# A TensorE loop whose leftover pairs become a short last round, ended by a branch

## The chip, the cores and the metric

One core of one Trainium2 chip. The metric is the device time of one execution in microseconds (us). "Before" and "after" are the kernel without and with the change. Times quoted for a kernel are medians of its fast runs. A ratio is the mean time of one kernel's fast runs over that of the other's of the same rounds, so it is not quite the ratio of the medians; each comes with a 95% interval.

## The reference, cut to what matters

```python
# x: (1, 512, 512, 192) bf16;  w: (1, 1, 4, 48, 48) bf16
xg = x.reshape(1, 512, 512, 4, 48)
out = einsum('bhwgc,gcd->bhwgd', xg, w[0, 0]).reshape(1, 512, 512, 192)
```

A grouped 1x1 convolution: 262,144 pixels of 192 channels in four groups of 48. 100.7 MB are read and 100.7 MB written, and there is little arithmetic.

## The kernel before

The pixels lie in 514 "groups" of four columns (128 partitions x 4 x 192 channels). Loads go to a ring of 240 columns, TensorE transposes a group and multiplies it by the weights, VectorE evicts the transposes, ScalarE evicts the products, and stores leave from a second ring. TensorE works in pairs of groups, 257 of them; a step transposes the next pair and multiplies this one: 24 matrix operations, each a weight load and a matmul, so 48 instructions (the page below counts 6,178 of each: 257 x 24, and ten for the weights).

The program of TensorE is not unrolled over all pairs. The ring repeats after 60 groups, so a body of 30 pairs can be a loop with fixed addresses:

```python
def loop_spans(units):
    body, out, run = RCOLS // 4, [], []              # body = 60 groups
    ...
            first = max((run[0].g0 - 1) // 2, 1)     # 9: the first pair that fits the pattern
            rounds, rest = divmod(run[-1].g1 - 2 * first - 2, body)   # 8 rounds, 14 groups left
            if rounds > 1:
                out.append((first + rest // 2, body // 2, rounds))    # (16, 30, 8)
    ...

            def step(pair):
                if pair + 1 < NP:
                    transposes(pair + 1)
                matmuls(pair)
            ...
            for first, body, rounds in LOOPS:
                for pair in range(pair, first):              # pairs 0 to 15, unrolled
                    step(pair)
                with pe.Fori(0, rounds):                     # 8 rounds of 30 pairs
                    for pair in range(first, first + body):
                        step(pair)
                pair = first + rounds * body
            for pair in range(pair, NP):                     # pair 256
                step(pair)
```

Pairs 0 to 8 have loads of odd sizes and cannot be in the loop. Pairs 9 to 15 could, but eight rounds of 30 leave seven pairs over, and these stand in front. All other engines run unrolled programs.

## Time and profile before

| | before |
|---|---|
| time, median of 3 (later of 12) | 477.2 us (477.3) |
| span in the profile | 475.5 us |
| bytes moved, mean rate | 201.57 MB, 424 GB/s |
| fetches of TensorE instructions, 16 KB each | 9 |

The windows of before by loop round: from:to, length, busy us of each engine with instruction counts, granted TensorE clock, DMA share, GB/s.

```profile
36.00:86.00 50.00, 49.03 (x727) 44.41 (x726) 29.13 (x31) 45.53 (x61) 2.00 (x4) 1.00 1.00 428
86.00:142.00 56.00, 49.85 (x719) 45.14 (x716) 28.38 (x31) 45.04 (x60) 0.93 (x2) 0.97 1.00 430
...
411.00:462.00 51.00, 49.47 (x726) 44.32 (x723) 29.25 (x31) 45.84 (x61) 0.00 (x0) 1.00 1.00 429
462.00:475.50 13.50, 1.23 (x14) 0.78 (x12) 0.00 (x0) 2.48 (x4) 0.00 (x0) 0.69 0.75 316
```

The DMA share is 1.00 or 1.01 in every round: the sixteen DMA engines bound the kernel. TensorE is busy too, but a round needs only 49 us of it and lasts up to 57. In the last 13.5 us the share falls to 0.75: some DMA engines are done before others, from 467.7 us on, as the last store's packets show (the last of them below). The kernel ends when the last of them ends.

The end of the timeline of before (start, length, what): TensorE is done, ScalarE issues the last store.

```profile
463.58 0.34 ACTq L427 DMA_DIRECT2D out_dram<-oring  x1
463.96 0.80 ACT L446 CAST oring<-o_ps 128x768 bf16<-128x768 f32 x1 [0.28 <-issue]
464.79 0.34 ACTq L427 DMA_DIRECT2D out_dram<-oring  x1
```

The last of its packets lands at 474.7 us, ten microseconds later: the store waits behind older ones. When it is issued, 2.96 MB of their packets have not ended, and the last of these ends at 473.7 us; its own first packet starts at 466.8. Three more things were read from the trace's records, one by one:

```
TensorE instruction fetches (queue 8, 16384 bytes each), start in us and length:
  18.24 0.97  26.46 1.03  36.94 0.95  45.31 0.88  54.03 0.88
  62.60 0.94  71.44 0.94  79.92 0.93  89.12 0.97       sum 8.47 us, mean 0.94
loop ends: register addition 36 to 42 ns; branch back, taken, 207 to 239 ns; not taken 76 ns
last store, 128 packets of 3072 bytes, ends of the last nine:
  473.74 | 473.85 473.97 474.09 474.21 474.32 474.44 474.56 474.68
```

The first eight fetches: 5.3 pairs or 255 instructions apart on average (1,787 matmuls and weight loads start between the first and the eighth). Below, a block is what one fetch brings, 16,384 bytes or about 256 instructions. The last eight packets of the last store come 0.12 us apart, after the other 120 are done: one engine (a sixteenth of 128 packets) alone ends the kernel.

### The profile page before, as it was taken

What the parts mean: (1) busy time and instruction counts of PE and PEld (TensorE: products, weight loads), DVE (VectorE), ACT (ScalarE), POOL (GpSimd) and SP (SyncE); (2) the same over time, 40 slices, a digit from 0 to 9 for tenths busy, and PEclk for the clock granted to TensorE, in tenths of its full rate; (3) what the DMA queues carried; (4) which work ended last, traced back from release to release, by engine and by line L of the source; (5) the groups of instructions that cost most, each with busy time, mean ns of one, the idle gap of its engine ahead of it and who ended that gap; (6) DMA issues with size and microseconds to landing.
All of it is one profiled execution on the core that took longest, in us unless ns stands there. A gap on an engine that the chain in (4) does not pass through costs nothing.

```text
span 475.5 us, 13580 instructions
## 1 busy us (share of the span) xinstructions
PE 427.4 (90%) x6178; PEld 386.3 (81%) x6178; DVE 246.8 (52%) x258; ACT 388.9 (82%) x515; POOL 12.5 (3%) x28
## 2 busy tenths in 40 slices
PE   5999999999698999999999897999698988999990
PEld 4988888888597988888888786888697877888870
DVE  2555565555354555555555543655354554555540
ACT  2899899998587998999998795898687868998890
POOL 1000000200002000000000000200002000000000
PEclk9999999999999999999999998999989999999996
DMA  8999999999999999999999999999999999999997
GB/s 326 439 393 421 435 426 429 442 416 433 435 434 428 435 421 435 435 429 435 429 434 432 430 432 430 432 430 428 433 433 428 433 429 427 428 435 428 423 429 307
DMA packets 10530, 201.57 MB, mean 424 GB/s; under 512 B 2096, under 2 KB 2096, under 8 KB 2608
## 3 DMA queue, kind: packets, MB, share of 16 engines
q1 hardware_dynamic: 4320, 97.44, 48.0%
q10 hardware_dynamic: 4976, 97.42, 47.9%
q0 software_dynamic: 1216, 6.49, 3.3%
q8 instruction: 9, 0.15, 0.1%
q14 instruction: 9, 0.07, 0.0%
HBM read 100.68 MB, written 100.66 MB: 423 GB/s over the span
## 4 chain that ended last, share of the span: by engine, by line
PE 61%; DMA 19%; ACT 12%; another core or an unknown queue 3%; issue 2%; ACTq 1%; SPq 0%; POOLq 0%
PE o_ps L370 35%; PE xT_ps L350 26%; ACT oring L446 12%; DMA out_dram<-oring 10%; DMA ring<-in_x_dram 9%; ACTq L427 1%; SPq L320 0%; SPq L313 0%; ACTq L420 0%; POOLq L300 0%; POOLq L299 0%; ACTq L429 0%
## 5 line engine op out<-in xcount | busy, mean ns | idle before, releaser
L446 ACT CAST oring<-o_ps 128x768 bf16<-128x768 f32 x514 | 387.6, 801 | 75.1 <-PE o_ps L370 47.0
L409 DVE COPY xT_sb<-xT_ps 128x1536 bf16<-128x1536 bf16 x257 | 246.1, 958 | 211.9 <-PE xT_ps L350 211.9
L370 PE MATMUL o_ps<-wt,xT_sb 128*128 128x144 bf16 (+1 forms) x3084 | 288.4, 235 | 25.1 <-ACT oring L446 20.6
L370 PEld LDWEIGHTS o_ps<-wt,xT_sb 128*128 128x128 bf16 x3084 | 211.6, 99 | 63.3 <-ACT oring L446 55.0
L350 PE MATMUL xT_ps<-ident,ring 128*128 128x128 bf16 x3084 | 220.4, 221 | 8.4 <-POOLq L300 4.3
L350 PEld LDWEIGHTS xT_ps<-ident,ring 128*128 128x128 bf16 x3084 | 188.3, 99 | 11.3 <-POOLq L300 4.5
L286 POOL DMA_DIRECT2D fill<-in_x_dram x8 | 4.6, 573 | 350.2 <-PE xT_ps L350 231.6
L296 POOL DMA_DIRECT2D ring<-in_x_dram x6 | 3.3, 560 | 0.0
L307 POOL DMA_DIRECT2D out_dram<-oring x6 | 3.3, 556 | 0.0
L332 PE MATMUL o_ps<-w_sb,esel 48*128 48x48 bf16 x10 | 0.6, 209 | 2.6 <-DMA w_sb<-in_w_dram 2.6
L332 PEld LDWEIGHTS o_ps<-w_sb,esel 48*128 48x128 bf16 x10 | 0.4, 111 | 2.5 <-POOL esel L273 2.5
L402 DVE CAST wt<-o_ps 128x480 bf16<-128x480 f32 x1 | 0.7, 657 | 3.2 <-PE o_ps L332 3.2
L446 ACT ACT_TABLE_LOAD x1 | 1.3, 1283 | 0.8 <-PEq L466 0.8
L273 POOL TENSOR_SCALAR_AFFINE_SELECT esel<-esel 48x272 bf16<-48x272 bf16 x1 | 0.4, 402 | 0.0
L270 POOL MEMSET esel<- 48x272 bf16 x1 | 0.3, 318 | 0.3 <-POOLq L466 0.3
L277 POOL TENSOR_SCALAR_AFFINE_SELECT ident<-ident 128x128 bf16<-128x128 bf16 x1 | 0.3, 282 | 0.0
L271 POOL MEMSET ident<- 128x128 bf16 x1 | 0.2, 198 | 0.0
L466 POOL MEMSET const-float32-0.0<- 128x1 f32 x1 | 0.1, 98 | 0.3 <-issue 0.3
L466 POOL MEMSET const-bfloat16-1.0<- 128x1 bf16 x1 | 0.1, 101 | 0.0
L466 POOL MEMSET const-uint8-127<- 128x1 uint8 x1 | 0.1, 101 | 0.0
L466 POOL MEMSET const-float32-1.0<- 128x1 f32 x1 | 0.1, 98 | 0.0
## 6 DMA issues: line engine op xcount, KB each, us to landing
ring<-in_x_dram SPq DMA_DIRECT2D x22, 3840.0 KB, 29.0
out_dram<-oring ACTq DMA_DIRECT2D x21, 3456.0 KB, 42.6
out_dram<-oring ACTq DMA_DIRECT2D x3, 2112.0 KB, 20.6
out_dram<-oring ACTq DMA_DIRECT2D x3, 1536.0 KB, 34.8
ring<-in_x_dram SPq DMA_DIRECT2D x2, 1536.0 KB, 35.0
out_dram<-oring ACTq DMA_DIRECT2D x1, 3072.0 KB, 37.9
out_dram<-oring ACTq DMA_DIRECT2D x1, 2688.0 KB, 37.5
ring<-in_x_dram SPq DMA_DIRECT2D x1, 2688.0 KB, 25.4
```

Of the source, the lines that this page charges most:

```text
L273: gp.affine_select(out=esel[:], in_=esel[:], pattern=[[-1, ECOLS]], compare_op=AluOpType.is_equal, fill=0.0, base=ESHIFT, channel_multipli ...
L286: gp.dma_start(dst, src).then_inc(fill_sem[k], 16)
L296: gp.dma_start(sbuf, dram).then_inc(ld_sem[ld_key[p.i, n]], 16)
L307: gp.dma_start(dram, sbuf).then_inc(st_sem[i][n], 16)
L332: last = pe.matmul(o_ps[:, NOB - 1, col:col + CG], lhsT=esel[:, s0:s0 + 128], rhs=w_sb[:, g, :], start=True, stop=True, skip_group_check=True)
L350: last = pe.transpose(xT_ps[:, g % NXP, j * 128:(j + 1) * 128], xg[:, j * 128:(j + 1) * 128], ident[:])
L370: last = pe.matmul(o_ps[:, v % NOB, c0_:c1_], lhsT=xs[:, j * 128:(j + 1) * 128], rhs=wt[:, WOFF[tc]:WOFF[tc] + (c1_ - c0_)], start=(tc == ...
L402: dve.tensor_copy(wt[:], o_ps[:, NOB - 1, 0:WCOLS]).then_inc(wc_sem, 1)
L409: dve.tensor_copy(xT_sb[pair % NXS][:, 0:n * 2 * UC].rearrange("p (g c) -> p g c", g=n), xT_ps[:, b0:b0 + n, 0:2 * UC]).then_inc(e_done[pa ...
L427: act.dma_start(dram, sbuf).then_inc(st_sem[i][n], 16)
L446: act.copy(out_columns(g).rearrange("p (u c) -> p u c", u=2), o_ps[:, v % NOB:v % NOB + 2, 0:UC]).then_inc(fa_done[g % (2 * NTOK)] if g < ...
L466: nc = _bacc.Bacc("TRN2", target_bir_lowering=False, num_devices=1)
```

## The change

The seven leftover pairs move into the loop. It begins at pair 9, has nine rounds, and the last ends after seven pairs by a branch. The intent is shorter code; the work and its order stay. Branches and register operations are the work of TensorE's sequencer, which the profile records apart from the matrix operations (the loop ends above: 36 to 42 ns and 76 to 239 ns).

```diff
             if rounds > 1:
-                out.append((first + rest // 2, body // 2, rounds))
+                out.append((first, body // 2, rounds, rest // 2))
...
-            for first, body, rounds in LOOPS:
+            for first, body, rounds, rest in LOOPS:
                 for pair in range(pair, first):
                     step(pair)
-                with pe.Fori(0, rounds):
-                    for pair in range(first, first + body):
+                with pe.Fori(0, rounds + 1) as i:
+                    for pair in range(first, first + rest):
                         step(pair)
-                pair = first + rounds * body
+                    with pe.If(i < rounds):
+                        for pair in range(first + rest, first + body):
+                            step(pair)
+                pair = first + rounds * body + rest
```

## The prediction

> **What bounds the kernel now.** The DMA engines. In the windows by stage, the DMA share is 1.00 from 36 to 462 us, at 428 to 433 GB/s. TensorE is next: where nothing holds it, a pair of groups takes 1.63 us (timeline, 20 to 26 us), so a round of 30 pairs would need 49 us; the rounds last 50 to 57. TensorE has some 30 us of slack over the span, spent in waits for evictions, loads and stores.
>
> **What the change removes, adds, moves.** The loop begins at pair 9 instead of 16 and makes 9 rounds instead of 8; seven pairs leave the unrolled code (336 of about 2,290 TensorE instructions, at 48 per pair). Work and order of all engines stay the same.
> - Removed: instruction fetches. The trace has 9 of 16 KB on one queue, from 18 to 89 us, each 0.88 to 1.03 us long and about 5.3 pairs (256 instructions) apart, none in later rounds. 336 instructions fewer should be one fetch fewer, perhaps two: about 0.9 us each of one DMA engine out of sixteen.
> - Added: per round, one comparison and one branch. In the trace a loop end costs the TensorE sequencer 36 ns for the addition and, for the branch, 207 to 239 ns when taken, 76 when not. The If should fall through in eight rounds, about 0.11 us each, and be taken once, 0.25 us; one more back edge is 0.3 us. Sum about 1.5 us of sequencer time. But the sequencer runs ahead: at the seven back edges of before, the gap between weight loads goes from its usual -15 ns to between -16 and +31 ns. TensorE should see below 0.3 us in all.
> - Moved: back edges come seven pairs earlier; the skip comes near 461 us.
>
> **How much is on the critical path.** Almost nothing. The added time sits in an engine with slack. The skip stands before the last pair, but the last store is issued at 464.8 and lands at 475.0, behind about 10 us of older stores, so a few us there would be hidden. A saved fetch counts only if its DMA engine finishes last: in the trace one engine ends at 474.7, the next by 473.9, so at most about 0.8 us can be gained.
>
> **Prediction.** 476.9 us (before 477.2), 8 in 10 between 475.8 and 478.4. Faster by over 2%: 0.01; within 2%: 0.95; slower by over 2%: 0.04.
>
> **What would show it.** 7 or 8 instruction fetches of 16 KB instead of 9, none after 90 us. Nine loop ends and nine more compare-and-branch records, eight near 76 ns and one near 210. Gaps of TensorE there under 0.1 us. DMA share still 1.00 in the rounds.
>
> **What would make it wrong.** [...] The body is 1,442 instructions and stays resident in before: no fetch after 89 us. After the change it begins elsewhere in its block and may touch seven blocks instead of six[...]. Fetches in every round would be the sign.

476.9 is 477.2 less 0.3 us for the saved fetch. Six or seven blocks for the body was the estimate: 1,442 instructions at about 256 a block, the spacing in the trace, are 5.6.

## More of the kernel before

The page of before. In the rows of digits each digit is the busy share of one of 40 slices in tenths; the queue lines give packets, MB and share of the 16 DMA engines' time.

```profile
span 475.5 us, 13580 instructions
PE 427.4 (90%) x6178; PEld 386.3 (81%) x6178; DVE 246.8 (52%) x258; ACT 388.9 (82%) x515; POOL 12.5 (3%) x28
...
DMA  8999999999999999999999999999999999999997
...
DMA packets 10530, 201.57 MB, mean 424 GB/s; under 512 B 2096, under 2 KB 2096, under 8 KB 2608
...
q8 instruction: 9, 0.15, 0.1%
q14 instruction: 9, 0.07, 0.0%
```

At each fetch's middle exactly 16 packets are in flight, the fetch being one of them: it holds one of the sixteen engines for about 0.94 us.

## The result, and the profile after

After: 476.42 us (476.24 to 476.88, 6 runs), before beside it 477.28 (6 runs); ratio 0.9981, 95% interval 0.9968 to 0.9993. That is 0.9 us or 0.2%: small, but clear of noise, and inside the predicted range. A second measurement (e8 below) gave 0.9983.

The page of after:

```profile
span 474.7 us, 13600 instructions
PE 430.2 (91%) x6178; PEld 389.4 (82%) x6178; DVE 246.8 (52%) x258; ACT 389.5 (82%) x515; POOL 12.5 (3%) x28
...
DMA  8999999999999999999999999999999999999997
...
DMA packets 10528, 201.54 MB, mean 425 GB/s; under 512 B 2096, under 2 KB 2096, under 8 KB 2608
...
q8 instruction: 7, 0.11, 0.1%
q14 instruction: 9, 0.07, 0.0%
```

The windows of after, over the same times as before (they no longer coincide with rounds):

```profile
36.00:86.00 50.00, 49.02 (x727) 44.39 (x725) 29.13 (x31) 45.64 (x61) 2.21 (x4) 1.00 1.00 427
86.00:142.00 56.00, 49.67 (x696) 45.21 (x694) 27.37 (x30) 43.51 (x59) 0.72 (x2) 0.94 1.01 431
...
411.00:462.00 51.00, 49.65 (x734) 44.80 (x732) 28.80 (x31) 45.59 (x61) 0.00 (x0) 1.00 1.00 427
462.00:475.50 13.50, 2.48 (x30) 1.68 (x27) 0.96 (x1) 3.87 (x6) 0.00 (x0) 0.68 0.75 316
```

The end of its timeline:

```profile
465.02 0.34 ACTq L431 DMA_DIRECT2D out_dram<-oring  x1
465.40 0.80 ACT L450 CAST oring<-o_ps 128x768 bf16<-128x768 f32 x1 [0.28 <-issue]
466.23 0.41 ACTq L431 DMA_DIRECT2D out_dram<-oring  x1
```

The reader should see three things. The only DMA traffic that differs is instructions: two packets and 0.03 MB less. The stages look as before, DMA share 1.00 or 1.01. And TensorE ends *later* in this profile: the last store is issued at 466.2 instead of 464.8, and yet the kernel ends earlier. That lateness is no effect of the change, though. In e8 below, the same kernel profiled again, the last store is issued at 463.96, earlier than in before:

```profile
463.14 0.80 ACT L450 CAST oring<-o_ps 128x768 bf16<-128x768 f32 x1 [0.28 <-issue]
463.96 0.35 ACTq L431 DMA_DIRECT2D out_dram<-oring  x1
```

So the gain does not need an earlier end of TensorE; whether its timing matters in another way is left to the experiments. Records of the same kind as before, from the profile of after:

```
TensorE instruction fetches: 18.06 26.09 36.74 43.51 54.27 62.47 71.29     sum 6.62 us, mean 0.95
new branch: falls through eight times, 77 to 84 ns; taken once, 208 ns (462.9 us)
loop ends: branch back taken eight times, 207 to 233 ns, then a register move of 29 to 38 ns at the head
gap between TensorE weight loads at the loop ends:
  before: -16 to +31 ns   after: +49 to +98 ns (one more stands in a wait of 5.5 us for a load)
gap at the new branch where it falls through: -36 to -14 ns, none
last store, ends of the last nine packets:
  473.60 473.60 473.63 473.66 473.72 473.72 473.74 473.78 473.86
```

The engine that ended alone is gone: the last packets now interleave, several engines end together. The end moved from 474.68 to 473.86 us, by 0.82 us, about the length of one fetch.

### The profile page after: what moved, and what is told of

Same layout as the page of the kernel before. It is cut to its first block, busy times and chain, and to the rows that moved or that the text cites. A ratio compares the mean times of both kernels' runs of the same rounds, so it can differ in the third digit from the quotient of the medians.

```text
span 474.7 us, 13600 instructions
## 1 busy us (share of the span) xinstructions
PE 430.2 (91%) x6178; PEld 389.4 (82%) x6178; DVE 246.8 (52%) x258; ACT 389.5 (82%) x515; POOL 12.5 (3%) x28
## 4 chain that ended last, share of the span: by engine, by line
PE 62%; DMA 20%; ACT 11%; another core or an unknown queue 2%; issue 2%; ACTq 1%; SPq 0%; POOLq 0%
PE o_ps L371 36%; PE xT_ps L351 26%; ACT oring L450 11%; DMA out_dram<-oring 10%; DMA ring<-in_x_dram 10%; ACTq L431 1%; SPq L321 0%; SPq L314 0%; ACTq L424 0%; POOLq L301 0%; POOLq L300 0%; ACTq L433 0%
```

## The experiments

Twelve runs were made, in three calls, each call on another chip; within a call they share a chip and the runs of before. All were correct. e8 is the changed kernel itself, the others are variants. The first theory, A: the gain is the instruction fetches saved on the DMA engine that ends last. Rival B: it comes from where the loop begins and from TensorE's changed timing.

| run | fetches | most on one of eight engines, if dealt in turn | median (range), us | ratio to before |
|---|---|---|---|---|
| after | 7 | 1 | 476.42 (476.24 to 476.88) | 0.9981 (0.9968 to 0.9993) |
| e8_after_again | 7 | 1 | 476.52 (475.94 to 476.62) | 0.9983 (0.9970 to 0.9997) |
| e4_if4 | 7 | 1 | 476.56 (476.53 to 476.69) | 0.9986 (0.9973 to 0.9999) |
| e2_front4 | 8 | 1 | 476.72 (476.08 to 478.20) | 0.9991 (0.9978 to 1.0003) |
| before | 9 | 2 | 477.28 to 477.38 | 1 |
| e12_front4pad | 9 | 2 | 477.42 (477.24 to 477.60) | 0.9998 (0.9986 to 1.0010) |
| e1_behind | 9 | 2 | 477.83 (477.08 to 478.66) | 1.0006 (0.9993 to 1.0019) |
| e3_front13 | 10 | 2 | 477.35 (476.98 to 477.58) | 1.0002 (0.9989 to 1.0015) |
| e5_front30 | 13 | 2 | 477.71 (477.48 to 477.99) | 1.0007 (0.9994 to 1.0021) |
| e9_front46 | 16 | 2 | 477.92 (477.32 to 478.32) | 1.0008 (0.9995 to 1.0021) |
| e10_front46pad | 17 | 3 | 478.67 (478.48 to 479.34) | 1.0025 (1.0013 to 1.0037) |
| e11_front51 | 17 | 3 | 478.93 (478.38 to 479.54) | 1.0029 (1.0015 to 1.0042) |
| e6_front67 | 20 | 3 | 479.32 (478.73 to 479.55) | 1.0039 (1.0026 to 1.0053) |
| e7_full | 48 | 6 | 483.48 (483.33 to 484.51) | 1.0128 (1.0112 to 1.0143) |

The fetches were counted in each profile. The third column is a theory; it is the count divided by eight, rounded up.

### e1_behind: no branch, the leftover behind the loop

```diff
-                with pe.Fori(0, rounds + 1) as i:
-                    for pair in range(first, first + rest):
-                        step(pair)
-                    with pe.If(i < rounds):
-                        for pair in range(first + rest, first + body):
-                            step(pair)
-                pair = first + rounds * body + rest
+                with pe.Fori(0, rounds):
+                    for pair in range(first, first + body):
+                        step(pair)
+                pair = first + rounds * body
```

> The loop begins at pair 9 as in the changed kernel, makes 8 rounds, and the seven leftover pairs stand unrolled behind it: no branch inside the loop, but the code is as long as in the kernel before. Theory A (the gain is the two instruction fetches of 16 KB less on the DMA engine that ends last): 8 or 9 fetches; with 9 the time is that of before, 477.2 (476.9 to 477.6), with 8 about 476.5. Rival B (the gain comes from where the loop begins and from TensorE's changed timing, not from fetches): 476.4, as after the change, with 9 fetches.

Nine fetches and 477.83 us; all five runs are above 477.0. Rival B expected 476.4 and falls: a loop that begins at pair 9 gains nothing when the code is as long as before. Two of the nine fetches came late here, at 458.0 and 467.9 us, since the code behind the loop is reached at the end. Theory A expected 476.9 to 477.6 with nine, so the median is 0.2 us above its range. In the profile two engines end the last store alone, at 475.5 and 475.9 us, and all others by 473.8. The late fetches may be why, but the records do not name engines and the interval of the ratio holds 1, so this is not shown.

### e2_front4, e3_front13: one fetch more, three fetches more

In both, the form of the change is kept and only the start of the loop moves:

```diff
-            first = max((run[0].g0 - 1) // 2, 1)
+            first = max((run[0].g0 - 1) // 2, 1) + 4      # e3: + 13
```

> The changed form with four more pairs in front (loop begins at pair 13, ninth round is three pairs). I expect 8 fetches, between the 7 of after and the 9 of before. Theory A with a second engine close behind (before, the last engine ended at 474.68 and the next at 473.74; a fetch occupies its engine 0.94 us on average): the first fetch saved gives nearly everything, so 8 fetches are as fast as 7, 476.3 to 476.7. A straight line through both would give 476.85. Rival B: 476.4 too or anything, not tied to the count.

Eight fetches, 476.72 us, about what theory A expected with a second engine close behind (476.3 to 476.7). The runs scatter widely, though (476.08 to 478.20), and in the profiled one the last store ended at 474.7 us like before, with one engine alone for the last 0.7 us, so this run alone decides little.

> The changed form with thirteen more pairs in front (loop begins at pair 22, seven full rounds and a short one of 24 pairs). I expect 10 fetches, one more than before. Theory A: one fetch more than before on the engine that ends last, 477.2 + 0.9 = 478.1 (477.7 to 478.5). Rival B: between 476.4 and 477.3, since the branch and the number of rounds are as in after or before.

Ten fetches, and 477.35 us where A expected 478.1: a miss. The tenth fetch cost nothing that can be seen, and in the profile two engines, not one, end the last store alone, at 474.58 and 474.68 us. Theory A as it stood, with every fetch on the one last engine, was in trouble.

### e4_if4: four branches in the round instead of one

```diff
-                    with pe.If(i < rounds):
-                        for pair in range(first + rest, first + body):
-                            step(pair)
+                    cuts = [first + rest + (body - rest) * q // 4 for q in range(5)]
+                    for lo, hi in zip(cuts, cuts[1:]):
+                        with pe.If(i < rounds):
+                            for pair in range(lo, hi):
+                                step(pair)
```

> The changed kernel with the 23 conditional pairs cut into four parts, each under its own branch: 27 more branches, of which 24 fall through (0.08 us each) and 3 more are taken near 463 us. Theory A and my prediction (branch time is hidden by the sequencer running ahead and by the DMA bound): 476.4 within 0.3, 7 fetches, gaps at the branches under 0.1 us. If branches cost what the sequencer records (24 x 0.08 + 3 x 0.25 = 2.7 us) on the critical path: 479.

Seven fetches and 476.56 us. Where the branches fall through there is no gap between weight loads (-36 to -14 ns, as between any two). At the end four branches are taken one after the other, 202 to 210 ns each, and here TensorE does wait. The timeline of this run, last pair and last store:

```profile
464.09 0.99 PE L371 MATMUL o_ps<-wt,xT_sb 128*128 128x144 bf16 x12 [0.86 <-ACT oring L452]
464.70 0.80 ACT L452 CAST oring<-o_ps 128x768 bf16<-128x768 f32 x1 [0.63 <-PE o_ps L371]
465.12 0.34 ACTq L433 DMA_DIRECT2D out_dram<-oring  x1
466.33 0.38 ACTq L433 DMA_DIRECT2D out_dram<-oring  x1
```

The idle time of 0.86 us before the last matmuls is put down to ScalarE. But the eviction that these matmuls wait for ended at 463.30 us, 0.76 us before the first weight load; the records of the four branches and of the loop end, 462.65 to 463.93 us, are what stands there. The expected "gaps under 0.1 us" therefore held for the 24 branches that fall through, not for these. The wait does not reach the end: the stores queue behind older ones, and the run is as fast as after. Branch time does not show in the kernel's time (476.56 us, after 476.42): in the rounds the sequencer runs ahead of TensorE, as the missing gaps show, and at the end the stores cover it (the last is issued at 466.33 us, the span is 474.8).

### e5_front30, e6_front67, e7_full: many fetches more

The same edit with 30 and 67 in place of 4; and in e7 no loop at all:

```diff
-            if rounds > 1:
+            if rounds > 99:
```

> The changed form with thirty more pairs in front (one whole round unrolled): 1,440 instructions more than after, I expect 12 or 13 fetches. The first four runs gave 7, 7, 8, 9, 10 and 9 fetches with 476.4, 476.6, 476.7, 477.3, 477.4 and 477.8, which is less than 0.94 us per fetch, so theory A splits. A1 (all fetches on the one engine that ends last, 0.94 us each): 480.5. A2 (fetches spread over many engines, or over an engine and its neighbours): 477.6. A3 (all on one engine, which has slack of up to 5 us at the end, since in before the first engines are done at 467.7 to 470.4): 477.3, no more than before.

> Sixty-seven more pairs in front: 3,216 instructions more than after, I expect 19 or 20 fetches. A1: 477.3 + 10.5 x 0.94 = 487. A2: 10.5 x 0.94 / 16 = 0.6 more than before, 478. A3: 487 less the slack of 4 to 6 us, 481 to 483.

> No loop: all 257 pairs unrolled, 10,080 instructions more than before, 39 more fetches, 48 in all. A1: 477.3 + 37 = 514. A2: 477.3 + 2.3 = 479.6. A3: 509. If the single late engine is made up for by nothing, the last 3072-byte packets of one engine end tens of us after the others under A1 and A3, and with them under A2.

A1 and A3 fall together: 48 fetches on one engine would have meant 509 us or more, and 483.48 were measured. e5 (477.71) fits A2 (477.6). But e6 and e7 cost more than A2, an even share over all sixteen engines, allows: 479.3 against 478, and 483.5 against 479.6. The fetches lie on several engines, but not on all. Lines of the page of e7:

```profile
span 482.8 us, 13563 instructions
...
DMA  8999999999999999999999999999999999999985
...
q8 instruction: 48, 0.79, 0.6%
```

How many engines? The packets of its last store say it:

```
e7, last store, 128 packets of 3072 bytes: 64 end by 475.08 us, none from there to 478.6, 64 after.
The last 8 of these end from 481.09 to 481.92, all others by 480.30.
```

Exactly half of the packets, so eight of sixteen engines, are done some five microseconds before the others. Six fetches on each of eight engines would hold each for 6 x 0.97 = 5.8 us, an estimate from the mean length of e7's own fetches. One engine ends another 1.6 us later. The last fetch of this run starts at 469.0 us, in the middle of the last stores; it probably holds that engine, but the records do not name engines, so this is argued and not shown. TensorE's own wait for instructions is not seen: in e7 every gap of over 60 ns between weight loads has a semaphore wait in it, and of its 4.0 us of idle time more than in before (37.5 against 33.5 us on the page) 3.9 are put down to ScalarE (24.5 against 20.6).

This gives theory A2s, the estimate from the 64 late packets of e7: fetches are dealt in turn to eight engines, and what counts is the largest number on one engine. It makes a sharp claim: time goes up in steps, at the ninth fetch and at the seventeenth, and little in between. That the turn is strict is an assumption here.

### e8_after_again

> The changed kernel again beside the same runs of before, to measure how firm its gain is: 476.4 within 0.3, ratio 0.997 to 0.999, 7 fetches. If it comes out at 1.000, the gain of the first measurement was chance and there is nothing to explain.

476.52 us and 0.9983: the gain is repeatable.

### e9 to e12: the steps, with padding that no engine executes

e9 and e11 move the start of the loop by 46 and 51. e10 is e9, and e12 is e2, with one more edit: the head of the loop is set to a fixed slot in its block of instructions, which puts padding in front of it, and a branch jumps over the padding (312 ns in e10). Shown is the edit of the loop's head; the start of the loop (+ 46 or + 4) and an import are left out:

```diff
-                with pe.Fori(0, rounds + 1) as i:
+                with nc.Fori(0, rounds + 1, engines=OrderedEngineSet([mybir.EngineType.PE]),
+                             head_slot={mybir.EngineType.PE: 100}) as i:
```

> Forty-six more pairs in front; 16 fetches expected. Eight runs so far: 7 fetches 476.4 to 476.6, 8 476.7, 9 and 10 477.3, 13 477.7, 20 479.3, 48 483.5. A1 and A3 have fallen (514 and 509 expected, 483.5 measured). At the end of the trace without a loop, eight engines finish near 475.0 and eight from 479.5 on: theory A2 in a sharper form, A2s: successive fetches go in turn to eight of the sixteen engines, so what counts is the largest number on one engine: 1 for 7 and 8 fetches, 2 for 9 to 16, 3 for 17 to 24, 6 for 48. A2s expects here, with two on each of the eight, no more than with 13: 477.5 to 478.0. Rival A2l, a straight line through the runs (0.16 us per fetch): 478.4.

> The same as with forty-six more pairs, but the head of the loop is set to slot 100 of its block of 256 instructions, so that some 140 to 210 slots of padding that no engine executes stand before it: 17 fetches expected, all executed instructions the same. A2s: a third fetch on one engine, 0.9 more than the run without padding, 478.4 to 478.9. A2l: 0.16 more. If unrolled pairs and not fetched bytes cost the time (rival R): the same as without padding.

> Fifty-one more pairs in front; 17 fetches expected. A2s: 0.9 more than with forty-six, 478.4 to 478.9, as the padded one. A2l: 0.16 more, as the padded one. R: 0.1 more, the padded one not.

> The changed form with four more pairs in front, which had 8 fetches and 476.7, with the head of the loop set to slot 100 of its block by padding: 9 fetches expected, all executed instructions the same. A2s: a second fetch on one engine, 477.2 to 477.6, the time of before. A2l: 476.9. R: 476.7.

The instruction lines of e9 and of e10:

```profile
q8 instruction: 16, 0.26, 0.2%
```

```profile
q8 instruction: 17, 0.28, 0.2%
```

e9, 16 fetches: 477.92 us, next to e5 with 13 (477.71). e10, 17 fetches: 478.67; its fastest run (478.48) is slower than the slowest of e9 (478.32), on the same chip. Only the padding and the one jump over it, on TensorE's sequencer, separate the two, so unrolled pairs as such (rival R) do not cost the time: the fetched block does. e11, also 17 fetches, agrees with 478.93. A straight line (A2l) expected 0.16 us from e9 to e10; 0.75 was measured, a step as A2s has it, if a little under 0.94.

One thing the expectation did not foresee: the added fetch does not come in the first pass. In e10 it starts at 377.5 us and in e12 at 138.9, 3.6 and 2.6 us after a branch back, in a later round of the loop. The last fetches of before, e3, e5, e6 and e11 also come after the first branch back, by 0.4 to 3.3 us; after, e8, e4, e2 and e9 have none there. Which kernels get such a fetch, and why, is open. In e10 and e12 no stall of TensorE for it can be seen: around the fetch every gap of over 0.1 us between weight loads has a semaphore wait in it. So both padded pairs test a fetch in a later round. That fetches of the first pass count too is seen in e9: its 16 are all of the first pass, and it is no faster than before, e3 and e5, which have one later fetch each.

e12 gives the change's own step back by padding alone: 476.72 (e2, 8 fetches) becomes 477.42 with 9, the time of before. It was expected at 477.2 to 477.6 by A2s, 476.9 by A2l and 476.7 by R. e2 and e12 ran in different calls and their intervals overlap, so this pair is weaker evidence than e9 and e10.

In the table the ratios form groups by the third column: 0.9981 to 0.9991, then 0.9998 to 1.0008, then 1.0025 to 1.0039, then 1.0128. The first step is 0.6 to 0.9 us, taken from eight fetches (476.72) or from seven (476.4 to 476.6) to nine (477.28 to 477.42); one fetch is 0.94. Where exactly it lies is less sure, since e2's interval of the ratio holds 1 and overlaps the neighbours on both sides. Within the second and the third group the ratio creeps up with the count, which A2s does not explain; with three to six runs each it cannot be told from noise here.

The kept traces allow one more test, which no expectation had named. In the last store each engine's packets follow one another: the next starts about 3 ns before the one before it ends. Linked so, the 128 packets fall into sixteen chains of eight, as sixteen engines would leave them (in e7 the linking is not clean). The latest ends of chains, in us, with a bar before the engines that should hold the largest number of fetches:

```
before,   9 fetches, one engine with two:    473.37 473.42 473.74 | 474.68
e12,      9, one with two:                   473.68 473.73 474.12 | 474.95
e3,      10, two with two:                   473.59 473.61 473.72 | 474.58 474.68
e5,      13, five with two:                  473.56 473.60 | 474.21 474.49 474.90 474.94 475.13
e9,      16, eight with two:                 472.73 473.46 | 474.21 474.51 474.52 474.60 474.89 475.20 475.43 475.46
e10,     17, one with three:                 474.78 474.85 475.13 | 476.74
e11,     17, one with three:                 475.11 475.13 475.58 | 476.94
e6,      20, four with three:                475.46 | 475.56 475.64 476.78 476.82
e1,       9, one with two:                   473.54 473.83 475.46 | 475.88
e2,       8, none with two:                  473.89 473.91 473.96 474.68
after,    7, none with two:                  473.72 473.72 473.78 473.86
```

Down to e11 the number of late engines is the one that A2s counts. e6 has two clearly late engines where it counts four, e1 two where it counts one (two of its fetches came after 458 us), and e2 one where it counts none. So the sharing over eight engines is well supported, and a strict turn is not shown in every run; the engines' ends also differ for other reasons, in after from 469.1 to 473.9 us.

No kernel's median is below that of after. A2s says why fewer than seven fetches should not help: one to eight fetches all leave one on the fullest engine. No kernel with fewer was run, so this is not shown.

## Why the prediction was right or wrong

- **What bounds the kernel**: right. DMA share 1.00 or 1.01 in the rounds of both. The end of TensorE does not set the time: in the two profiles of the changed kernel it lies at 465.0 and 462.7 us, on both sides of before's 463.5, and both spans are shorter than before's.
- **Removed fetches**: right in number, "one fetch fewer, perhaps two": two, 7 instead of 9, none after 71 us. The reason given, 336 instructions fewer, accounts for one, 7 instead of 8 in the first pass. The other is the fetch that before makes in its second round; the prediction took it for one of the first pass ("none in later rounds"), and why it goes away is open.
- **Where they count**: right in kind. The prediction said that a saved fetch counts only if its engine ends last, and gave 0.8 us as the most. Measured were 0.9 us, nearly a whole fetch. The term that was mis-sized is this one: the forecast of 476.9 holds only 0.3 us for it, between nothing and 0.8, and the prediction did not say which engine fetches. The runs put in its place that fetches are shared out over eight engines (in e7 64 of the last store's 128 packets are late): before had nine, so by A2s one engine had two, and the change took that second one away. That the saved fetch lay on the engine that ended last was luck as far as the prediction goes. By A2s the second fetch saved should earn nothing; e2, with eight, is at 0.9991 between after and before, so this is open.
- **Branch time**: right that it is hidden; e4 with 27 branches more has the same time (476.56 us, after 476.42). In detail TensorE lost a little more than "below 0.3 us in all": the loop ends now leave gaps of 49 to 98 ns, about 0.5 us over the seven that can be read, counting each against the usual -15 ns. The register move at the loop head, which the prediction did not list, may be the cause; no run tests it.
- **Records**: right. Nine loop ends, nine new branches, eight at 77 to 84 ns and one at 208.
- **The skip near the end**: right. Even 0.86 us of idle TensorE there (e4) did not reach the last store's landing.
- **The fear of fetches in every round**: did not happen: in after, a loop body of some 1,440 instructions, more than five blocks, runs eight more rounds after the first, the last of them short, with no fetch (the last starts at 71.3 us, the first branch back at 74.0). How much code would bring them was not shown by any run. The fear was not idle, though. Before itself has one fetch in its second round, and e10 and e12 have one each later on.

## What to carry to other kernels

When DMA bounds a kernel and its engines end unevenly, look at what the last engine carries besides data: here an instruction block of 16 KB was worth 0.9 us, and unrolling everything cost 1.3%. In this kernel short code paid off by the fetch and not by the instruction, and from 16 to 17 fetches in a step of 0.75 us, so count the fetches in the profile before cutting code, and stop when no fetch on the last engine is left to save. Branches on TensorE, which has slack here (some 49 us of work in rounds of 50 to 57) and whose sequencer runs ahead, cost nothing that can be seen (e4, 27 more: 476.56 us, after 476.42).
